# Regrouping 24 units of linear attention feeding a gated product, with two more transposes on the DMA queue and a reordered opening

## The chip, the cores and the metric

The kernel runs on one core of one Trainium2 chip. The metric is device time in microseconds (us), the median of several executions. "Span" is the time that the profiler shows for one execution, some 2 us less.

## The reference

Linear attention with a decay per head, in float32, for 4 batches x 8 heads x 768 positions x 64 dimensions, feeds a bilinear layer over 3072 tokens. In outline, not word for word:

```python
for b in range(nb):                      # blocks of 64 positions
    intra = (qb @ kb.T * Dmask) @ vb     # Dmask: lam ** (i - j) for i >= j
    inter = (qb * lam_pow) @ kv_state
    out[:, :, sl] = intra + inter
    kv_state = lam_block * kv_state + (kb * rev_pow).T @ vb
# ... cut: x = out as 3072 tokens x 512
return (x @ w_a) * (x @ w_b) @ w_out     # 512 -> 1536 -> 512
```

## The kernel before

A **unit** is 128 tokens, so there are 24. For each, the kernel scales q and k (`P`: GpSimd, called POOL below), transposes them (`T` on TensorE from unit 5, or by a transposing DMA from unit `DMA_T_FROM`), forms scores and masks them (`S`), updates and copies the recurrent state (`V`), and forms the attention output (`O`, `O2`; `Q` does it for two units along with the scores of the next two). Then **groups** of one to four units go together through the a and b products (96 matmuls as wide as the group), and unit by unit through the output product. `PLAN` hangs the attention pieces of coming units into slots of the running group; a slot is one of 12 a/b steps, or half an output row later on.

```python
GROUPS = (4, 1, 2, 4, 4, 4, 4, 1)
LOOKAHEAD = (3, 2)
DMA_T_FROM = 9
PLAN = {
    # ... cut: groups 0 and 1
    2: [(0, "V", 6), (1, "T", 7), (1, "P", 8), (4, "T", 8), (4, "P", 9), (6, "S", 7),
        (6, "S", 8), (7, "V", 7), (6, "P", 10), (10, "V", 8),
        (12, "Q", (7, 8, 9, 10)), (12, "P", 11), (13, "V", 9), (14, "P", 12),
        (14, "O2", (9, 10))],
    3: [(3, "S", 11), (3, "S", 12)],     # ... cut: a loop fills groups 3 to 5
}
# ... cut
def prep_k(u):
    make_ks(u, "dve" if u < n0 + 2 else "pool")
    make_qs(u, "pool")
    used["u"] = u + 1
    if u >= DMA_T_FROM:
        qkT = qkT_pool.tile([128, 2, HP, 128], BF16, name="qkT", tag="qkT")
        nc.sync.dma_start_transpose(out=..., in_=...)      # shortened

def prep_v(u):
    make_vb(u, "pool" if u < n0 + 3 else "dve")   # bf16 cast of the values
    pump()                                        # issues the loads that are due
# ... cut
def pieces_O(us, nxt=()):
    kqs = [score_banks() for u in nxt]
    for u in us:
        inter(u)                # full products, 128 x 128 weights
    for u, kq in zip(nxt, kqs):
        scores(u, kq)           # 64-row weights
    for u in us:
        intra(u)                # weights with 64 columns
        xT, col = xTs[u]
        evac_o(u, xT, col)
    if len(us) == 2 and us[0] >= n0 + 5:
        kv_beside(us[1])
    for u, kq in zip(nxt, kqs):
        masks(u, kq)
    # ... cut: state copy
# ... cut: the last row of the last group goes out in pieces of 256, 128, 128 columns
warm(13, 512)                   # idle matmuls while the first loads arrive
# ... cut
for u, at in enumerate((4, 5, 2, 6)):
    U[u]["o"] = ps_bank("o_ps", [128, HP, 128], F32, at=at)
intra(0, True)
evac_o(0, *xTs[0])
intra(1, True)
inter(1)
evac_o(1, *xTs[1], eng="dve")
intra(2, True)
intra(3, True)
inter(2)
evac_o(2, *xTs[2], eng="dve")
inter(3)
evac_o(3, *xTs[3])
```

## Time and profile before

| | before |
|---|---|
| median (lowest to highest), 3 runs | 233.85 us (233.6 to 234.01) |
| profiled span | 231.8 us |
| first a/b matmul starts | 18.59 us |
| TensorE's last matmul ends | 228.69 us |
| last row lands in memory | 230.74 us |

TensorE is busy 97% of the span, so the page is read from TensorE outwards: what each of its matmuls costs from start to start, and what it waits for. The prediction shows those views. Two landmarks split the rest: up to the first a/b product ("the opening") TensorE waits for loads, scalings and casts; after its last matmul ("the tail", 2.05 us here) the last row must be copied and stored.

TensorE's timeline of the opening's end, kernel before (start, busy us, engine, line, operation, shape, count):

```profile
15.36 0.50 PE L366 MATMUL kvd<-vb,scratch 128*128 128x128 bf16 x6
15.79 0.64 PE L352 MATMUL o_ps<-m,vb 128*64 128x128 bf16 x16
16.36 0.40 PE L342 MATMUL o_ps<-scratch,st 128*128 128x128 bf16 x4
16.69 0.68 PE L352 MATMUL o_ps<-m,vb 128*64 128x128 bf16 x16
17.30 0.62 PE L342 MATMUL o_ps<-scratch,st 128*128 128x128 bf16 x8
```

Products with weights of 128\*64 and of 128\*128 take turns: four changes of form (the shape of the weights) from the first line to the last. Four full products at 56 ns would take 0.22 us; from 16.36 to 16.69 they took 0.33.

### The profile page before, as it was taken

Reading aid. Unit: us, or ns where it says so; the run is one execution under the profiler, and the core shown is the slowest. Engines: PE = TensorE matmul, PEld = TensorE weight load, DVE = VectorE, ACT = ScalarE, POOL = GpSimd, SP = SyncE. Lnnn points to the kernel's source line nnn. Section 1 sums busy time; section 2 is a strip of 40 time slices with the busy share of each in tenths; the row PEclk is TensorE's granted clock in tenths of the full one; section 3 lists DMA queues with packets and bytes.
Section 4 is the critical chain, followed back from the end, with each engine's and each line's share of the span. In section 5 each row is a group of like instructions: output and inputs, shape, how many; then the busy total and the mean of one; then the engine's idle time right before and its main releaser. Section 6 shows DMA issues by size and latency. Waiting matters only on the chain.

```text
span 231.8 us, 4520 instructions
## 1 busy us (share of the span) xinstructions
PE 225.2 (97%) x1775; PEld 124.6 (54%) x1775; DVE 115.9 (50%) x204; ACT 91.1 (39%) x172; POOL 50.6 (22%) x65
## 2 busy tenths in 40 slices
PE   7799999999999999999999999999999999999994
PEld 2474444449698554454544454544454544444494
DVE  0896566636469726684334484235583323332050
ACT  3585754066463342333233332333332233332251
POOL 6070000248373333445000543001200000000000
PEclk9999999999999999999999999999999999999999
DMA  4999999999999999998759997229300220000311
GB/s 151 303 283 351 348 364 293 295 207 223 185 225 176 224 208 209 209 197 190 270 189 200 220 182 121 91 96 205 65 3 0 91 93 0 1 0 5 130 49 48
DMA packets 96389, 38.84 MB, mean 168 GB/s; under 512 B 83312, under 2 KB 91888, under 8 KB 96368
## 3 DMA queue, kind: packets, MB, share of 16 engines
q1 hardware_dynamic: 96224, 38.54, 72.9%
q8 instruction: 14, 0.23, 0.4%
q14 instruction: 7, 0.06, 0.1%
q10 hardware_dynamic: 144, 0.00, 0.0%
HBM read 28.32 MB, written 6.29 MB: 149 GB/s over the span
## 4 chain that ended last, share of the span: by engine, by line
PE 92%; DMA 3%; ACT 2%; SPq 1%; DVE 0%; issue 0%
PE a_ps L435 27%; PE b_ps L435 27%; PE op L467 27%; DMA k<-in_k_dram 3%; PE o_ps L352 3%; PE kq L310 2%; PE o_ps L342 2%; PE kvd L366 2%; PE tps L296 1%; ACT o_kept L458 1%; SPq L209 1%; PE kq L578 1%; ACT xT L359 0%; PE kv L366 0%; PE tk L542 0%; DVE scratch L531 0%
## 5 line engine op out<-in xcount | busy, mean ns | idle before, releaser
L447 DVE TENSOR_TENSOR ab<-a_sb,b_ps 128x512 bf16<-128x512 bf16 (+2 forms) x96 | 52.3, 552 | 77.9 <-PE b_ps L435 56.9
L435 PE MATMUL a_ps<-xT,wa_sb 128*128 128x512 bf16 (+2 forms) x384 | 77.2, 326 | 0.6 <-ACT xT L359 0.6
L435 PE MATMUL b_ps<-xT,wb_sb 128*128 128x512 bf16 (+2 forms) x384 | 77.2, 326 | 0.0
L442 ACT CAST a_sb<-a_ps 128x512 bf16<-128x512 f32 (+2 forms) x96 | 45.6, 481 | 63.1 <-PE a_ps L435 61.5
L467 PE MATMUL op<-wo_sb,ab 128*128 128x512 bf16 (+2 forms) x312 | 65.6, 363 | 0.0
L435 PEld LDWEIGHTS <-wb_sb 128*128 128x128 bf16 x384 | 34.5, 98 | 28.7
L435 PEld LDWEIGHTS <-wa_sb 128*128 128x128 bf16 x384 | 33.7, 98 | 29.1 <-POOL wa_sb L162 0.6
L467 PEld LDWEIGHTS <-ab 128*128 128x128 bf16 x312 | 28.8, 98 | 29.9
L327 DVE TENSOR_TENSOR m<-kq,lotri 128x512 bf16<-128x512 f32 x47 | 29.3, 682 | 18.1 <-PE kq L310 17.8
L259 POOL TENSOR_TENSOR qk<-kf,lp_k 128x512 bf16<-128x512 f32 x18 | 18.9, 1049 | 74.7 <-DMA kf<-in_k_dram 47.3
L264 POOL TENSOR_TENSOR qk<-qf,lp_q 128x512 bf16<-128x512 f32 x20 | 22.0, 1099 | 23.4 <-DMA qf<-in_q_dram 23.4
L462 ACT COPY o_sb<-op 128x512 f32<-128x512 f32 (+2 forms) x19 | 10.3, 541 | 34.0 <-PE op L467 34.0
L359 ACT CAST xT<-o_ps 128x512 bf16<-128x512 f32 x22 | 12.0, 590 | 17.9 <-PE o_ps L352 17.5
L398 DVE TENSOR_TENSOR st<-kvd,bdiag 128x512 bf16<-128x512 f32 x18 | 12.3, 682 | 4.9 <-PE kvd L366 3.8
L273 DVE CAST vb<-vf 128x512 bf16<-128x512 f32 x17 | 9.4, 553 | 0.0
L298 ACT COPY qkT<-tps 128x1024 bf16<-128x1024 bf16 x5 | 5.1, 1012 | 9.9 <-PE tps L296 9.9
L197 PE MATMUL idle<-idle_sb 128*128 128x128 bf16 (+1 forms) x31 | 7.2, 372 | 1.3 <-DVE idle_sb L192 1.3
L352 PE MATMUL o_ps<-m,vb 128*64 128x128 bf16 x192 | 7.9, 222 | 0.0
L273 POOL CAST vb<-vf 128x512 bf16<-128x512 f32 x7 | 4.7, 666 | 14.0 <-DMA vf<-in_v_dram 14.0
L342 PEld LDWEIGHTS <-st 128*128 128x128 bf16 x80 | 5.4, 98 | 2.8
L310 PE MATMUL kq<-qkT 64*128 64x128 bf16 x160 | 6.6, 218 | 0.0
L352 PEld LDWEIGHTS <-vb 128*64 128x64 bf16 x192 | 5.8, 109 | 1.4
(57 smaller groups left out, 87.4 us busy)
## 6 DMA issues: line engine op xcount, KB each, us to landing
vf<-in_v_dram SPq DMA_DIRECT2D x24, 256.0 KB, 4.9
qf<-in_q_dram SPq DMA_DIRECT2D x20, 256.0 KB, 4.4
kf<-in_k_dram SPq DMA_DIRECT2D x20, 256.0 KB, 4.6
out_dram<-o_sb SPq DMA_DIRECT2D x16, 256.0 KB, 2.0
wst<-in_moe_w_a_dram SPq DMA_DIRECT2D x6, 512.0 KB, 8.7
wst<-in_moe_w_b_dram SPq DMA_DIRECT2D x6, 512.0 KB, 8.8
wst<-in_moe_w_out_dram SPq DMA_DIRECT2D x6, 512.0 KB, 8.5
out_dram<-o_kept SPq DMA_DIRECT2D x7, 256.0 KB, 2.5
```

The source lines that it names most:

```text
L259: eng_of(eng).tensor_mul(qk[:, 1], raw.pop((u, "k")), lp_k[:, u % NB].to_broadcast([128, H, D]))
L264: eng_of(eng).tensor_mul(U[u]["qk"][:, 0], raw.pop((u, "q")), lp_q[:, u % NB].to_broadcast([128, H, D]))
L273: eng_of(eng).tensor_copy(vb, vf)
L310: nc.tensor.matmul(kq[i][:, hp, :], lhsT=d["kT"][p, hp, :], rhs=d["qT"][p, hp, :], start=True, stop=True, skip_group_check=True)
L327: nc.vector.tensor_mul(m, kq[i], lotri_bc)
L352: nc.tensor.matmul(d["o"][p, hp, :], lhsT=d["vb"][:, 2 * hp + i, :], rhs=d["m"](i, hp), start=(first and hp == 0), stop=True, skip_group_c ...
L359: nc.scalar.copy(xT[:, :, col:col + BLK], o_ps)
L398: nc.vector.tensor_mul(st[:].rearrange("p hp i d -> p hp (i d)"), ps[:].rearrange("p hp i d -> p hp (i d)"), bdiag_bc)
L435: nc.tensor.matmul(ps[:, :gt], lhsT=w_sb[:, s, f * 128:(f + 1) * 128], rhs=xT[:, s, :gt], start=(s == 0), stop=(s == KS - 1))
L442: nc.scalar.copy(a_sb[:, :gt], ps[:, :gt])
L447: nc.vector.tensor_mul(ab[:, f, :gt], a_sb[:, :gt], ps[:, :gt])
L467: nc.tensor.matmul(op[:, lo:hi], lhsT=ab[:, f, t * 128:(t + 1) * 128], rhs=wo_sb[:, f, lo:hi], start=(f == 0), stop=(f == FC - 1))
```

## The change

Its intent: take 16 transposes off TensorE by giving units 7 and 8 to the DMA queue, spread the deadlines of units 7 to 12 by groups of 2, 2 and, at the end, 3, and shorten the opening by ordering its products, masks and evacuations so that less waits for the last values.

```diff
-GROUPS = (4, 1, 2, 4, 4, 4, 4, 1)
+GROUPS = (4, 1, 2, 2, 4, 4, 4, 3)
-DMA_T_FROM = 9
+DMA_T_FROM = 7
 # ... cut
-    2: [(0, "V", 6), (1, "T", 7), (1, "P", 8), (4, "T", 8), (4, "P", 9), (6, "S", 7),
-        (6, "S", 8), (7, "V", 7), (6, "P", 10), (10, "V", 8),
-        (12, "Q", (7, 8, 9, 10)), (12, "P", 11), (13, "V", 9), (14, "P", 12),
-        (14, "O2", (9, 10))],
-    3: [(3, "S", 11), (3, "S", 12)],
+    2: [(0, "V", 6), (1, "P", 8), (4, "P", 9), (9, "P", 10), (10, "S", 7), (10, "S", 8),
+        (11, "V", 7), (13, "P", 11), (14, "O2", (7, 8)), (15, "P", 12)],
+    3: [(1, "S", 9), (1, "S", 10), (2, "V", 9), (5, "Q", (9, 10, 11, 12)), (6, "P", 13),
+        (8, "V", 11), (9, "P", 14), (12, "O2", (11, 12))],
+    4: [(3, "S", 13), (3, "S", 14)],
 }
-for _g, _u in ((3, 11), (4, 15), (5, 19)):
+for _g, _u in ((4, 13), (5, 17)):
 # ... cut: the last groups' slots; qkT buffers 5 -> 6; LOOKAHEAD switches one unit earlier
-        if len(us) == 2 and us[0] >= n0 + 5:
+        if len(us) == 2 and us[0] >= n0 + 3:
             kv_beside(us[1])
 # ... cut: the same condition for its state copy
-    for u in range(n0):
+    for u in range(n0 - 1):
         make_vb(u, "pool")
 # ... cut
-    for hps in ((0, 1), (2, 3)):
-        for u in range(3):
-            kv_part(u, hps)
-            if hps[0]:
-                kv_copy(u, sts[u], ("act", "act", "dve")[u])
+    make_vb(3, "pool")
+    for u in range(2):
+        kv_part(u, (0, 1))
+    for u in range(2):
+        kv_part(u, (2, 3))
+        kv_copy(u, sts[u], "act")
+    kv_part(2, range(HP))
+    kv_copy(2, sts[2], "dve")
 # ... cut
     intra(2, True)
+    inter(2)
+    evac_o(2, *xTs[2])
     intra(3, True)
-    inter(2)
-    evac_o(2, *xTs[2], eng="dve")
     inter(3)
-    evac_o(3, *xTs[3])
+    xT, col = xTs[3]
+    o3 = U[3].pop("o")
+    nc.scalar.copy(xT[:, 0:2, col:col + BLK], o3[:, 0:2])
+    nc.vector.tensor_copy(xT[:, 2:4, col:col + BLK], o3[:, 2:4])
```

More of the change, by code (lines that the diff above doesn't have):

```diff
@@ L57 @@
          (12, "P", _u + 5), (13, "V", _u + 2), (16, "Q", (_u + 2, _u + 3, _u + 4, _u + 5))])
-PLAN[3] += [(_s, "W", None) for _s in range(12, 19)]
-PLAN[5] = [(_s, _n, (21, 22, 23) if _us == (21, 22, 23, 24) else _us)
-           for _s, _n, _us in PLAN[5] if _us != 24]
-PLAN[6] = [(4, "O", 23)]
+PLAN[4] += [(_s, "W", None) for _s in range(9, 16)]
+PLAN[6] = [(1, "P", 23), (4, "V", 21), (7, "Q", (21, 22, 23)), (12, "O", 23)]
 @with_exitstack
@@ L93 @@
     prep_pool = ctx.enter_context(tc.tile_pool(name="prep", bufs=6))
-    qkT_pool = ctx.enter_context(tc.tile_pool(name="qkT", bufs=5))
+    qkT_pool = ctx.enter_context(tc.tile_pool(name="qkT", bufs=6))
     msk_pool = ctx.enter_context(tc.tile_pool(name="msk", bufs=4))
@@ L182, in pump @@
                     return
-            elif c >= used["u"] + LOOKAHEAD[used["u"] > 9]:
+            elif c >= used["u"] + LOOKAHEAD[used["u"] > 8]:
                 return
@@ L424, in pieces_O @@
             masks(u, kq)
-        if len(us) == 2 and us[0] >= n0 + 5 and us[1] % NB < NB - 1:
+        if len(us) == 2 and us[0] >= n0 + 3 and us[1] % NB < NB - 1:
             kv_copy(us[1], kv["ps"])
```

## The prediction

> **What bounds the kernel now.** I read the page's shares first, then who waited for whom on TensorE, then the chain of waits, then single stretches of the timeline. Busy shares and slices of the page:
>
> ```profile
> span 231.8 us, 4520 instructions
> PE 225.2 (97%) x1775; PEld 124.6 (54%) x1775; DVE 115.9 (50%) x204; ACT 91.1 (39%) x172; POOL 50.6 (22%) x65
> ...
> PE   7799999999999999999999999999999999999994
> ...
> PEclk9999999999999999999999999999999999999999
> DMA  4999999999999999998759997229300220000311
> ```
>
> TensorE is busy in every slice but the first two and the last (a slice is 5.8 us); no other engine passes 50%. The DMA row is full up to slice 18 (about 104 us): no bound while TensorE stays full, but the resource the change leans on. TensorE's complete list of waits (us in total, times, longest):
>
> ```profile
> PE idle L197 <- DVE idle_sb L192: 1.3, 1, 1.3
> PE tq L542 <- DVE scratch L531: 0.8, 4, 0.2
> PE tk L542 <- DVE scratch L531: 0.7, 2, 0.4
> PE a_ps L435 <- ACT xT L359: 0.6, 2, 0.5
> PE tn L562 <- ACT scratch L553: 0.2, 1, 0.2
> ```
>
> All of it lies before 18.6 us except 0.2 us at 51.8. So after the opening only fewer TensorE cycles save time, and any new wait costs its full length. What a kind of matmul costs is its pace, not its listed duration, for these overlap. From the chain of waits (start, us, what):
>
> ```profile
> 62.78 0.44 PE a_ps L435 x4
> 63.22 0.44 PE b_ps L435 x4
> ...
> 64.75 0.45 PE tps L296 x8
> ...
> 84.69 0.86 PE b_ps L435 x4
> ```
>
> Four 512-column matmuls pace 0.864 us (216 ns each), four 256-column ones 0.437 (109 ns), eight 128-column transposes 0.45 (56 ns). In the one-unit group the timeline has four 128-column products every 0.224 us (56 ns).
>
> **What the Trainium skill says.** "TensorE: Matmul & The Clock Gate", section "Wait — 56ns, not 53.3ns?", gives 55.6 ns start to start for 128 columns and 215.7 for 512 when warm; the trace agrees (56, 216). The same page under "Back-to-back issue gap" gives about 81 and 131 ns for load-and-multiply streams; the trace contradicts that, and I use the trace. "Advanced Engine Details and Errata", "X-Bar Transpose (TRN2)", says a transposing DMA runs about as fast as a plain one; 15 of them here take a median 4.3 us to land and, in the saturated stretch, add about 0.85 us to the landing series (73.26, 74.09, 74.94), against 1.15 for a 256 KB load. Fair agreement.
>
> **The change, part by part.**
>
> 1. *Groups.* Old: five groups of 4, one of 2, two of 1. New: four of 4, one of 3, two of 2, one of 1. Each group has 96 a/b matmuls of its width. Old: 5 x 96 x 0.216 + 96 x 0.109 + 2 x 96 x 0.056 = 103.7 + 10.5 + 10.8 = 125.0 us. New: 4 x 20.7 + 96 x 0.163 (384 columns, an estimate between the measured widths) + 2 x 10.5 + 5.4 = 82.9 + 15.6 + 21.0 + 5.4 = 124.9 us. The output products are per unit, unchanged. Worth 0: narrow groups are not inefficient here. What moves is deadlines: units 7 and 8 alone are due at about 83 us, and 9 to 12 at about 101, where now 7 to 10 are due at 83.66 and 11 to 14 at 119.
>
> 2. *Units 7 and 8 by DMA.* Removes 16 transposes x 56 ns = **0.90 us** of TensorE, on the path, and two 1.01 us evacuations of ScalarE, off it. Adds two transposing DMAs. For unit 8 the state update goes from 4 to 8 half-size products; the timeline has both at about 0.22 us, so 0.
>
> 3. *Opening.* The stretch that ends it, from the timeline of before:
>
> ```profile
> 15.08 0.62 POOL L273 CAST vb<-vf 128x512 bf16<-128x512 f32 x1 [0.47 <-DMA vf<-in_v_dram]
> ...
> 15.40 1.51 ACT L396 CAST st<-kv 64x256 bf16<-64x256 f32 x4 [0.50 <-PE kv L366]
> 15.66 1.16 POOL L325 TENSOR_TENSOR m<-scratch,lotri 128x512 bf16<-128x512 bf16 x1
> ...
> 17.95 0.59 ACT L359 CAST xT<-o_ps 128x512 bf16<-128x512 f32 x1 [0.43 <-PE o_ps L342]
> ...
> 18.59 1.89 PE L435 MATMUL a_ps<-xT,wa_sb 128*128 128x512 bf16 x8 [0.45 <-ACT xT L359]
> ```
>
> Now: unit 3's values are cast ahead of the POOL mask, so the mask ends at 16.82; ScalarE's state copies start at 15.40; the last evacuation is one 0.59 us cast. After: the mask can start when its source is done (14.90) and ends at 16.07, the cast at 16.69. Unit 0's and 1's products precede unit 2's, so the copies run 14.90 to 16.40. The 24 products run without the pause for unit 2's values, ending near 15.5 instead of 15.7. Unit 2 then goes through at 16.4 to 16.9, unit 3 at 16.9 to 17.4. DVE (masks to 16.21, state 0.68, unit 1's 0.69) is free at 17.6, ScalarE (units 0 and 2, 0.59 each) at 17.6; the two halves take about 0.37 (ScalarE's 256-column cast) and 0.42. The first a_ps starts near 18.1: **0.5 us** gained. Weights allow it: the second a-chunk is cast by 21.48, needed at 22.27 - 0.5; the second b-chunk by 23.34, needed at 23.99 - 0.5. Both just hold.
>
> 4. *What is given back.* I followed the order of issue on the DMA queue, with the landings that the trace matches to each issue. Two transposes more, at 2.1 us each of the queue's issuing, come ahead of units 11 and 12. Estimates from loads landing 3.6 to 4.9 us after issue, two scalings of 1.04 us on POOL, then the transpose (4.8 us): unit 7 lands at 65.6 and 8 at 71.1 (their scores come at about 71.7); unit 12's values at 81.0 (78.9 before); its transpose at 87 (86.1 before). In the second group of two, VectorE has unit 12's cast ahead of everything: done at 81.5 to 81.9. Then two products (0.35), four masks at 0.61 us pace, a product, a state copy and two products bring it to 86.7 to 87.1, when the accumulator of slot 4 comes free. TensorE, at the packed pace, wants that bank for unit 9's output at about 86.3. So a **new wait of 0.4 to 0.8 us**, say 0.6; unit 12's scores follow near 88, just after its transpose. Sum: -0.90 - 0.5 + 0.6 = -0.8 us; 233.85 - 0.8 = 233.05. I go to 232.9, as a slot plan tuned on the chip would probably have taken out part of that wait.
>
> **The rivals.**
>
> - *No new wait.* TensorE stayed full before with loads just ahead of it: 72 us from 40 to 112 with 71.83 busy. If VectorE gets through in time, the gain is 1.4 us: 232.4. For it: deadlines of 9 and 10 move later. Against it: four masks and a state copy now sit in a phase where slots are 0.87 us, not 1.73.
> - *The DMA queue becomes the bound between 70 and 90 us.* A transpose waits in line for POOL and holds up every load behind it:
>
> ```profile
> SPq L282 <- POOL qk L264: 5.5, 7, 2.7
> ...
> SPq L282 <- POOL qk L259: 1.4, 1, 1.4
> ```
>
>   Should values 12 or transpose 12 land 1.5 us later than estimated, VectorE, in order, and then TensorE stop as long: 234.4. Lateness would have to reach 5 us for a loss of 2%.
> - *The opening gains nothing*, because weights set the pace there: 233.4 with the wait of point 4. Against it: above, both chunks still come first.
>
> **Range and chances.** Transposes -0.9 are sure to within 0.1; the opening is -0.5, give or take 0.3; the wait 0 to 1.5. Hence 231.8 to 234.1. A gain over 2% needs 4.7 us, three times all that I can find; a loss over 2% needs a stall of 6. So 0.01, 0.97, 0.02.
>
> **What would show it.** Transposes on TensorE 24 instead of 40 after the opening, DMA transposes 17 instead of 15; a_ps first at about 18.1; a/b time unchanged in sum; TensorE's waits with a new entry of 0.4 to 0.8 us between 82 and 90, on VectorE or a bank, and no other. Wrong if the opening's a_ps doesn't move, if TensorE waits for a transpose or a cast held by its load, or if TensorE idles at a group's edge or in the three-unit tail.

## The result, and the profile after

The changed kernel took 234.21 us (233.88 to 235.01, five runs) against 233.85 in the same rounds. Executions over 1.5% slower than the fastest of the same kernel are left out of the means. Ratios here are the mean time of one kernel's runs over the mean of the other's of the same rounds, so not quite the ratio of these medians: 1.0023, with a 95% interval of 1.0002 to 1.0044. So nothing was gained: 1.3 us more than the 232.9 predicted, just above the range.

The page of the kernel after, busy shares and slices:

```profile
span 232.4 us, 4469 instructions
...
PE 223.3 (96%) x1742; PEld 127.6 (55%) x1763; DVE 115.6 (50%) x204; ACT 89.6 (39%) x171; POOL 50.6 (22%) x65
...
DMA  4999999998999999999999629990222000220012
```

TensorE's busy sum is 1.9 us less, yet the span is 0.6 us longer. The sum is no measure here: 21 matmul records are missing in this trace (1742; the kernel e1 below, with the same instructions in another order, shows 1763, and 225.3 us busy), so I read starts. The DMA row stays full up to slice 21 but for one 8; before, it had a dip to 8, 7, 5 in slices 18 to 20 (the first slice is 0). TensorE's waits, kernel after (us in total, times, longest):

```profile
PE kq L308 <- DMA qkT<-qk: 0.5, 1, 0.5
...
PE o_ps L340 <- DVE ab L445: 0.4, 1, 0.4
```

These two are new: one score block waits for a transposing DMA, one output accumulator for VectorE. Both are between 86 and 89 us. (The view also has 0.5 us of "issue" ahead of output products; e1, with all records, has none.) TensorE's timeline there, kernel after:

```profile
87.48 0.61 PE L340 MATMUL o_ps<-qkT,st 128*128 128x128 bf16 x8 [0.44 <-DVE ab L445]
88.03 0.40 PE L308 MATMUL kq<-qkT 64*128 64x128 bf16 x8
88.90 0.40 PE L308 MATMUL kq<-qkT 64*128 64x128 bf16 x8 [0.48 <-DMA qkT<-qk]
```

The eight score matmuls at 88.03 are unit 11's, those at 88.90 unit 12's. Busy times overlap, so a bracket understates a pause. From the starts of the single matmuls in the trace, 0.60 us was lost before 87.48 and 0.65 before 88.90. Another 0.09 goes at 82.5 to a change of form: from the last 256-column a/b product to the first score product it is 0.205 us, against 0.109 within the form. The changed kernel has 40 changes after its first a/b product, the kernel before 39. Together 1.34 us. The chain of waits says why unit 12 was late (start, us, what):

```profile
76.70 4.61 DMA kf<-in_k_dram
...
81.46 1.04 POOL qk L257
82.51 1.19 POOL qk L262
83.72 5.14 DMA qkT<-qk
```

Unit 12's keys land at 81.30, POOL scales k and q, the transpose is issued at 83.72 and lands at 88.86. VectorE's timeline, kernel after, explains the other wait:

```profile
82.30 0.49 DVE L271 CAST vb<-vf 128x512 bf16<-128x512 f32 x1 [2.12 <-DMA vf<-in_v_dram]
82.71 0.74 DVE L445 TENSOR_TENSOR ab<-a_sb,b_ps 128x256 bf16<-128x256 bf16 x2
83.37 2.47 DVE L325 TENSOR_TENSOR m<-kq,lotri 128x512 bf16<-128x512 f32 x4
...
86.09 0.68 DVE L396 TENSOR_TENSOR st<-kvd,bdiag 128x512 bf16<-128x512 f32 x1
86.70 1.07 DVE L445 TENSOR_TENSOR ab<-a_sb,b_ps 128x256 bf16<-128x256 bf16 x3
```

VectorE stands idle for 2.12 us ahead of unit 12's cast, whose values come by the same queue. Then everything queues: two products, four masks, a product, the state, and the product that frees the accumulator.

The opening, PE and evacuation rows of the timeline of the kernel after:

```profile
15.85 0.64 PE L350 MATMUL o_ps<-m,vb 128*64 128x128 bf16 x16
16.42 0.40 PE L340 MATMUL o_ps<-scratch,st 128*128 128x128 bf16 x4
16.75 0.41 PE L350 MATMUL o_ps<-m,vb 128*64 128x128 bf16 x8
...
17.77 0.40 PE L340 MATMUL o_ps<-scratch,st 128*128 128x128 bf16 x4
18.20 0.37 ACT L638 CAST xT<-o_ps 128x256 bf16<-128x256 f32 x1
18.61 0.42 DVE L639 CAST xT<-o_ps 128x256 bf16<-128x256 f32 x1 [1.06 <-ACT xT L638]
18.62 1.91 PE L433 MATMUL a_ps<-xT,wa_sb 128*128 128x512 bf16 x7 [0.24 <-ACT xT L638]
```

The attention products start no earlier (15.85 for 15.79), now change form six times instead of four, and the two halves of the last evacuation run one after the other. The first a/b matmul starts at 18.62.

The accounts of the two profiled executions, from starts of matmuls and landings of stores in the traces:

| term | predicted | measured |
|---|---|---|
| opening (first a/b start) | -0.5 | +0.03 (18.59 to 18.62) |
| transposes on TensorE | -0.90 | -0.89 (2.23 to 1.34 us in all) |
| a/b time of the groups | 0 | 0 (96 of 384 columns took 15.60 us, estimated 15.6) |
| wait for VectorE at an accumulator | +0.6 | +0.60 |
| wait for unit 12's transpose | 0 | +0.65 |
| one more change of form, at 82.5 | 0 | +0.09 |
| TensorE's last matmul | -0.8 | +0.48 (228.69 to 229.17) |
| tail (last matmul to last landing) | not priced | +0.17 (2.05 to 2.22) |

### The profile page after: what moved, and what is told of

It is laid out like the page before. It is cut to its first block, busy times and chain, and to the rows that moved or that the text cites. A ratio compares the mean times of both kernels' runs of the same rounds, so it can differ in the third digit from the quotient of the medians.

```text
span 232.4 us, 4469 instructions
## 1 busy us (share of the span) xinstructions
PE 223.3 (96%) x1742; PEld 127.6 (55%) x1763; DVE 115.6 (50%) x204; ACT 89.6 (39%) x171; POOL 50.6 (22%) x65
## 4 chain that ended last, share of the span: by engine, by line
PE 85%; DMA 8%; SPq 2%; ACT 1%; issue 1%; POOL 1%; DVE 0%; POOLq 0%; ACTq 0%
PE a_ps L433 26%; PE b_ps L433 25%; PE op L465 24%; DMA k<-in_k_dram 3%; PE o_ps L350 3%; DMA qkT<-qk 2%; PE kq L308 2%; DMA kf<-in_k_dram 2%; PE o_ps L340 2%; PE kvd L364 1%; SPq L280 1%; ACT o_kept L456 1%; SPq L207 1%; PE tps L294 1%; POOL qk L262 1%
## 5 line engine op out<-in xcount | busy, mean ns | idle before, releaser
L445 DVE TENSOR_TENSOR ab<-a_sb,b_ps 128x512 bf16<-128x512 bf16 (+3 forms) x96 | 52.3, 552 | 75.9 <-PE b_ps L433 68.4
L433 PE MATMUL a_ps<-xT,wa_sb 128*128 128x512 bf16 (+3 forms) x377 | 76.6, 325 | 0.8 <-ACT xT L638 0.2
L433 PE MATMUL b_ps<-xT,wb_sb 128*128 128x512 bf16 (+3 forms) x382 | 77.0, 325 | 0.1
L440 ACT CAST a_sb<-a_ps 128x512 bf16<-128x512 f32 (+3 forms) x96 | 45.7, 481 | 65.9 <-PE a_ps L433 54.9
L465 PE MATMUL op<-wo_sb,ab 128*128 128x512 bf16 (+2 forms) x300 | 64.2, 362 | 0.9 <-issue 0.5
L433 PEld LDWEIGHTS <-wb_sb 128*128 128x128 bf16 x384 | 36.0, 98 | 26.6
L433 PEld LDWEIGHTS <-wa_sb 128*128 128x128 bf16 x384 | 35.3, 98 | 27.3 <-issue 0.8
L262 POOL TENSOR_TENSOR qk<-qf,lp_q 128x512 bf16<-128x512 f32 x20 | 21.5, 1074 | 22.9 <-DMA qf<-in_q_dram 22.9
L296 ACT COPY qkT<-tps 128x1024 bf16<-128x1024 bf16 x3 | 3.0, 1012 | 8.9 <-PE tps L294 8.9
```

Source lines behind the costliest of these rows:

```text
L262: eng_of(eng).tensor_mul(U[u]["qk"][:, 0], raw.pop((u, "q")), lp_q[:, u % NB].to_broadcast([128, H, D]))
L433: nc.tensor.matmul(ps[:, :gt], lhsT=w_sb[:, s, f * 128:(f + 1) * 128], rhs=xT[:, s, :gt], start=(s == 0), stop=(s == KS - 1))
L440: nc.scalar.copy(a_sb[:, :gt], ps[:, :gt])
L445: nc.vector.tensor_mul(ab[:, f, :gt], a_sb[:, :gt], ps[:, :gt])
L465: nc.tensor.matmul(op[:, lo:hi], lhsT=ab[:, f, t * 128:(t + 1) * 128], rhs=wo_sb[:, f, lo:hi], start=(f == 0), stop=(f == FC - 1))
```

## The experiments

Kernels sent together shared a chip and its runs of the kernel before, whose medians were 233.63 to 233.82. The theory: what the transposes gave was paid back as waits around 82 to 90 us, because the DMA queue now carries two more transposes ahead of unit 12; the opening's term does not exist. A rival: the loss lies elsewhere (the groups, the tail, the added DMA itself), and the waits are only where it surfaces.

### e1: unit 12's deadline two slots later

```diff
-    3: [... (5, "Q", (9, 10, 11, 12)), (6, "P", 13),
+    3: [... (6, "P", 13), (7, "Q", (9, 10, 11, 12)),
```

> The changed kernel with one edit: in the fourth group the combined piece for units 9 to 12 comes after slot 7 instead of slot 5, 1.75 us later. Theory A (the transpose of unit 12, which landed at 88.86 us, and VectorE, late by 0.60 us, stop TensorE by 1.34 us in all between 82 and 90 us): both waits vanish, the scores of unit 12 come near 89.5 us, and the time is 234.2 - 1.2 = 233.0 us. Rival B (the loss lies elsewhere, or the masks of units 11 and 12, now later, stop TensorE before the output piece of slot 12): 234.2 us, or a new wait after 90 us.

Both waits between 82 and 90 went, and TensorE ended at 228.19 instead of 229.17: 0.98 us, for 1.25 of waits and 0.05 in the opening, less two new pauses of 0.16 at 91.1 and 91.7, where ScalarE's two evacuations and VectorE's masks and state stand ahead of the next casts and products. But the time was 233.82 (233.25 to 233.95), ratio 0.9991 (0.9977 to 1.0006): the same as before. TensorE's gain was lost after its end: the tail took 2.91 us. By the timelines of the output stores, the first of the last five was issued 0.98 us earlier than in the changed kernel (223.60 for 224.58), but the last only 0.27 (229.37 for 229.64): its issuing was held up. The DMA records name the cause. TensorE fetches its own instructions by DMA, 16 KB as one packet, 14 times in an execution. In e1 one such fetch took one of the 16 DMA engines from 227.09 to 228.91. Of the 128 packets (2 KB) of row 22's store, 120 had started by 227.76, the last eight only from 228.90; the store took 4.27 us to land instead of 2.0, and the last row's three pieces stood behind it. So the theory held for TensorE, and there was a second place of loss that I had not priced.

### e2: unit 12's cast on POOL

```diff
-        make_vb(u, "pool" if u < n0 + 3 else "dve")
+        make_vb(u, "pool" if u < n0 + 3 or u == 12 else "dve")
```

> The changed kernel with the cast of unit 12's values on POOL instead of VectorE, which sat idle 2.12 us for that load and then came to the masks late. Theory A (what ends the stall is the landing of unit 12's transpose near 88.9 us; the VectorE wait lies in front of it and is absorbed): the wait of the output product falls from 0.60 us start to start to 0.3 or less, the wait for the transpose grows by as much, and the time stays at 234.2 within 0.15 us. Rival C (each wait costs on its own): 0.4 to 0.6 us less, 233.7 us.

234.24 us (233.81 to 235.01), ratio 1.0018 (1.0000 to 1.0036). The time is as expected, but not for the reason expected: both waits were shorter, 0.35 us for VectorE and 0.5 for the transpose from start to start, as the transpose also landed earlier (88.39), and TensorE ended 0.47 us earlier; a tail of 2.70 took that back. This can't be put down to the edit: run again (r1 below), the unedited changed kernel also waited only 0.38 us for VectorE. What the run does show is that 0.35 us stays with the cast gone. Four masks, a product, the state and a product still stand on VectorE from 83.03 on, ahead of the accumulator.
Whether a shorter VectorE wait alone would be absorbed by the transpose stays undecided, because the transpose moved too.

### e4: units 7 and 8 transposed on TensorE again

```diff
-DMA_T_FROM = 7
+DMA_T_FROM = 9
-    2: [(0, "V", 6), (1, "P", 8), (4, "P", 9), ...
+    2: [(0, "V", 6), (1, "T", 7), (1, "P", 8), (4, "T", 8), (4, "P", 9), ...
```

> The changed kernel with its groups, but units 7 and 8 transposed by TensorE as before. Theory A: the DMA queue has two transposes less ahead of unit 12, whose transpose lands near 86 to 87 us; both waits fall to under 0.3 us together (-1.1), the 16 transposes cost 0.89 us: 234.0 us, no different from either kernel within 0.3. Rival D (the four masks in slots of 0.87 us are the cause, whatever the queue does): the VectorE wait of 0.6 us remains, and the time is 234.5 us or more.

234.0 us (233.93 to 234.11), ratio 1.0004 (0.9991 to 1.0017). Unit 12's transpose landed at 86.54 instead of 88.86, TensorE's wait for it disappeared, and the wait for VectorE was 0.35 us: so rival D was right about that much, whatever the queue does, and the other 0.25 of the changed kernel's 0.60 goes with the late cast (its masks began at 83.37, those of e2 and r1 at 83.03 and 83.00). TensorE ended at 229.37, 0.20 later than in the changed kernel: in this pair of executions, of the 0.89 us that the two DMA transposes take off TensorE some 0.7 came back. Two executions of the changed kernel itself ended 0.23 apart, so this is rough. Part of the 2.3 us by which unit 12's transpose moved is scatter: with the changed kernel's order of the queue it landed between 87.08 (x3) and 88.86 in nine executions. So the two transposes account for 0.5 to 2.3, if e4's single landing is typical.

### e5 and x8: the two DMA transposes in the old groups

e5 is the kernel before with `DMA_T_FROM = 7`, six qkT buffers, and the scores of units 7 and 8 two slots later:

```diff
-    2: [(0, "V", 6), (1, "T", 7), (1, "P", 8), (4, "T", 8), (4, "P", 9), (6, "S", 7),
-        (6, "S", 8), (7, "V", 7), (6, "P", 10), (10, "V", 8),
+    2: [(0, "V", 6), (1, "P", 8), (4, "P", 9), (8, "S", 7),
+        (8, "S", 8), (9, "V", 7), (6, "P", 10), (10, "V", 8),
```

> The kernel before with its groups (4,1,2,4,4,4,4,1) and units 7 and 8 transposed by DMA, their scores moved from slot 6 to slot 8 of the third group. The 16 transposes are worth -0.89 us. Theory A (two more transposes in the DMA queue set everything behind them back by about 3 us): the transpose of unit 10 lands near 77.5 to 78.2 us, but its scores are due near 75.5 us, so TensorE waits 1.5 to 2.5 us there and the time is 234.4 to 235.4 us. Rival (the queue catches up, as the DMA engines had slack): 232.95 us.

234.52 us (234.03 to 234.92), ratio 1.0032 (1.0016 to 1.0049). The waits view of e5:

```profile
PE kvd L366 <- DVE st L398: 1.4, 1, 1.4
```

That is a stall of my own making: the slot shift put two state copies behind four masks on VectorE. It says nothing of the queue. x8 takes it out: unit 8's state update goes beside its output products, as in the changed kernel.

```diff
-        (8, "S", 8), (9, "V", 7), (6, "P", 10), (10, "V", 8),
+        (8, "S", 8), (9, "V", 7), (6, "P", 10),
-        if len(us) == 2 and us[0] >= n0 + 5:       # twice
+        if len(us) == 2 and us[0] >= n0 + 3:
```

> As e5_dma_only (groups of the kernel before, units 7 and 8 by DMA), but the state update of unit 8 comes beside its output, as in the changed kernel, so that two state copies no longer follow each other behind four masks, which is where e5_dma_only lost 1.5 us. Theory A: the transpose of unit 10 lands near 77.4 us and its scores are due near 76.9 us: a wait of 0.3 to 1 us, in all 233.8 - 0.9 + 0.3 to 1 = 233.2 to 233.9 us. If the DMA queue has slack here: 232.9 us.

234.03 us (233.44 to 234.68), ratio 1.0015 (0.9999 to 1.0032). Its waits view:

```profile
PE kq L310 <- DMA qkT<-qk: 1.2, 2, 0.8
```

With the old groups TensorE waits for transposes of units 9 and 10, which now land at 76.31 and 77.56. So in either grouping tried, the DMA transposes' 0.89 us turns into waits for later transposes.

### e6: the new opening alone

The kernel before with the opening's lines of the diff above, and nothing else.

> The kernel before with the new opening alone (order of products, cast after the mask on POOL, split evacuation). The prediction on record gave it 0.5 us: 233.35. What the two traces suggest instead: the new order alternates six times instead of four between full products and products with 64 columns of weights, each alternation 0.20 us start to start instead of 0.03 to 0.06, and that eats the gain: 233.85 within 0.15 us, first a_ps product no more than 0.1 us from 18.59.

233.76 us (233.64 to 234.11), ratio 0.9996 (0.9981 to 1.0011); the first a/b matmul started at 18.47. The opening is worth nothing that these runs resolve. (The 0.20 us in the expectation is a misreading: by the starts in both traces, the change from one form to the other takes 0.15 us for 128-column products, against 0.056 within a form, so it costs 0.09.)

### x3: the instruction fetches shifted

If fetches come after a fixed count of TensorE instructions, more and shorter idle matmuls at the start must move them all. From e1:

```diff
-    warm(13, 512)
+    warm(48)          # 48 of 128 columns
```

> The changed kernel with the combined piece at slot 7, and 48 idle matmuls of 128 columns instead of 13 of 512 in the wait for the first load: 70 more TensorE instructions, so that each instruction fetch of 16 KB comes some 35 matmuls earlier. Theory E: the last fetch (at 227.09 us, 1.82 us long) held one DMA engine with its share of row 22's store, whose last eight packets started at 228.90, and the last store landed 2.9 us after TensorE's end where the kernel before took 2.05. Now the fetch comes near 222 us, the last landing is about 2.05 us after TensorE's end, and the time is 233.8 - 0.85 = 232.95 us. Rival F (two full stores and three pieces so close together are slow by themselves): the last landing stays 2.7 to 2.9 us after TensorE's end, 233.8 us.

232.85 us (232.82 to 232.91), ratio 0.9962 (0.9949 to 0.9976): 0.97 us below e1's median, or 0.7 by the two ratios, as the two ran on different chips, with TensorE's end unmoved (228.20 against 228.19). The last fetch came at 222.18 instead of 227.09, and the tail was 1.94. The spread of six executions fell from 0.70 us to 0.09. So the tail of the three-unit group was a collision of a store with a fetch, shown by moving the fetches alone.

### x7: another shift

From e1, a shift by 13 matmuls instead of 35:

```diff
-    warm(13, 512)
+    warm(26, 256)
```

> The changed kernel with the combined piece at slot 7 and 26 idle matmuls of 256 columns: 13 more, so the last fetch comes some 13 matmuls earlier than the one at 227.09 us, near 226.2 us, and if it takes 1.0 to 1.8 us ends at 227.2 to 228.0. It still holds one engine's share of row 22's store, but that engine has time to catch up before the last piece. Theory E: row 22's store lands 1 us late or so, the last landing is 1.95 to 2.3 us after TensorE's end, time 232.9 to 233.2 us. Rival F (the position of the fetch doesn't matter): 233.8 us.

232.88 us (232.83 to 232.89), ratio 0.9962 (0.9950 to 0.9974); the last fetch came at 225.35 and was over at 226.30, between the bulk of two stores (the first landed in 2.16 us instead of 2.02), and the tail was 1.94. It is the fetch's place, not the number of idle matmuls.

### x5: the same shift in the kernel before

> Control: the kernel before with the same 48 idle matmuls instead of 13 wide ones. Its last fetch (227.62 us) ends just ahead of its first output piece, and its last landing is 2.05 us after TensorE's end. If the edit acts only through the last fetch, nothing changes here: 233.8 us within 0.2, last landing 2.0 to 2.1 us after TensorE's end, first a_ps product within 0.1 us of 18.59. If the edit is worth something by itself (warmer clock, earlier fetches elsewhere), this is faster too.

The edit is that of x3, in the kernel before. 234.68 us (234.19 to 234.99), ratio 1.0040 (1.0024 to 1.0056): 0.9 us slower by the ratio, not unchanged as expected. As a control it failed, but it showed what the reordered opening is good for. The first fetch now came at 13.63 instead of 18.18 and delayed unit 3's values to 16.13 (15.03 before). POOL's and TensorE's timeline, x5 (old opening):

```profile
16.18 0.61 POOL L273 CAST vb<-vf 128x512 bf16<-128x512 f32 x1 [1.56 <-DMA vf<-in_v_dram]
16.76 1.15 POOL L325 TENSOR_TENSOR m<-scratch,lotri 128x512 bf16<-128x512 bf16 x1
17.96 0.49 PE L352 MATMUL o_ps<-m,vb 128*64 128x128 bf16 x11 [0.91 <-POOL m L325]
```

The same rows for x3 (new opening), whose values were as late (16.39):

```profile
14.99 1.15 POOL L323 TENSOR_TENSOR m<-scratch,lotri 128x512 bf16<-128x512 bf16 x1 [0.38 <-ACT scratch L322]
16.44 0.61 POOL L271 CAST vb<-vf 128x512 bf16<-128x512 f32 x1 [0.30 <-DMA vf<-in_v_dram]
```

In the old order the mask stands behind the late cast and TensorE waits, to an a/b start of 19.69; in the new order the mask is done first, and the start is 18.60. The new opening saves 1.1 us when values are late, and nothing when they are not.

### x6, and both again: the shift in the changed kernel

> The changed kernel with nothing but the 48 idle matmuls (the fetches come some 35 matmuls earlier; the combined piece stays at slot 5). Its waits for VectorE and for the transpose, 1.34 us, should remain, and only the tail should change: last landing 1.94 instead of 2.22 us after TensorE's end, so 234.2 - 0.3 = 233.9 us, and runs closer together than the 1.1 us over which those of the changed kernel spread, if the spread comes from the last fetch. If the 1 us gained by x3_fetch against the late piece alone came from something else in the body, this run too would gain about 1 us: 233.2 us.

The edit is that of x3, in the changed kernel. 233.26 us (233.10 to 233.62), ratio 0.9980 (0.9969 to 0.9992): more gain than the tail alone should give. So I ran the changed kernel and x6 once more, together on another chip.

> The changed kernel, unedited, on the same chip and in the same rounds as the next run. Expected: 234.2 us within 0.3, spread of 0.8 us or more among its runs; waits for VectorE and the transpose of unit 12 of 1.2 to 1.4 us start to start together; last fetch within 1.2 us of TensorE's end and a last landing 2.2 to 2.9 us after it.

> x6_after_fetch again, unedited, beside the changed kernel. Its profiled run was the slowest of its five (233.62 against 233.26). If the tail is all that the shifted fetches change, it is 0.3 to 0.9 us faster than the changed kernel beside it, the size of that kernel's tail over 1.94 us, with the same waits of about 1.2 us in the body. If the fetches also free the body, the waits fall to 0.8 us or less.

The changed kernel again: 234.09 us (233.21 to 234.87), ratio 0.9997 (0.9973 to 1.0021). x6 again: 233.17 us (233.15 to 233.29), ratio 0.9970 (0.9953 to 0.9987). The difference of 0.92 us lies in two places. The profiled tails of the changed kernel were 2.22 and 3.20, those of x6 both 1.94. And the wait for unit 12's transpose varied: 0.65 and 0.79 us in the changed kernel, 0.83 and 0.13 in x6, as the transpose landed at 88.86, 88.62, 88.66 and 87.92. In the first of these a fetch at 84.82 lasting 1.31 us delayed the load of unit 13's values, queued just ahead of the transpose: it landed 5.76 us after its issue, against the usual 4.6. That may make up to 1.1 us of unit 12's lateness. But the kernel before has such a fetch too (at 83.94, with unit 12's transpose landing 5.89 us after its issue), so it is nothing new; and in x6 no fetch lies there, and it was still late once; a fetch at 81.08 delayed unit 11's landing. What moves this landing by a microsecond is left open. The wait for VectorE was 0.60 us in the first of the four executions and 0.35 to 0.38 in the other three.

### x4: everything that helped

From x3, `intra(2)` ahead of `inter(1)` in the opening, so that the products change form four times instead of six:

```diff
     intra(1, True)
+    intra(2, True)
     inter(1)
     evac_o(1, *xTs[1], eng="dve")
-    intra(2, True)
     inter(2)
```

> As x3_fetch, and in the opening unit 2's 64-column products go ahead of unit 1's full products: four alternations between the two kinds instead of six. At 0.15 us each over the normal pace this is 0.3 us of TensorE, of which a wait for the POOL mask (ends 16.2 us) and for ScalarE's evacuation of unit 2 may take back half: first a_ps product 0.1 to 0.3 us earlier than in x3_fetch, time 232.65 to 232.85 us if the last fetch stays clear of the stores. If alternation isn't the cost, no difference.

232.78 us (232.72 to 232.90), ratio 0.9960 (0.9945 to 0.9975). The first a/b matmul started at 18.42 instead of 18.60, and TensorE ended 0.17 earlier. The 44 attention products took 1.92 us from first to next block, against 2.15 in the changed kernel. TensorE then waited 0.3 us for the cast of the first weight chunk, so here the weights set a floor at about 18.4 (that cast began at 17.75, against 17.25 in the changed kernel). This version is faster than the kernel before, by 0.85 us on the same chip: its interval excludes 1, and it is still under 1%. It was not run beside the changed kernel.

## Why the prediction was wrong

The time stayed within 2%, as foreseen, but no gain of 0.9 us came. Three steps failed and one term was left out, each worth some tenths and all in the same direction. Two of the text's own signs of being wrong came: the opening's first a/b product did not move, and TensorE waited for a transpose.

**Right by their own working.** Transposes: -0.89 against -0.90. Groups: 0, with the 384-column estimate at 15.60 us. The wait for VectorE, 0.60 of "0.4 to 0.8", at the accumulator of unit 9's output and for the reason given: cast, masks and state in order on VectorE, ahead of a product. (The cast was done at 82.8, not 81.5 to 81.9.) So this much of the trade was priced as it came in the profiled execution: 0.9 off, 0.6 back. The size was partly luck: in three other executions of the same plan the wait was 0.35 to 0.38, and e2 and e4 show 0.35 without the late cast. Masks, state and products make that much without it.

**Point 3, the opening: predicted -0.5, measured +0.03.** Two of its sentences failed. "The 24 products run without the pause for unit 2's values, ending near 15.5": there was no such pause. The stretch from the first of these products to the first attention product took 1.60 us in both traces. The 0.26 us that this is over 24 times 0.056 lies, in both kernels, in a pause of 0.16 after the second product, where a mask of VectorE ends just before TensorE goes on (14.43 and 14.47 in the kernel before), and in a change of form at the end: 0.15 us from the last product of one form to the first of the next, against 0.056 within a form. And "unit 2 then goes through at 16.4 to 16.9" counted products, not changes; two more cost 0.19. The working is then +0.06 for the start, +0.19 for the changes, -0.22 because the last evacuation before the first a/b product is a half (0.37 for 0.59): +0.03. x4 shows the term by removing two changes: -0.18. The Trainium skill could have told me: "TensorEngine Tiling (Array Packing)", "Key Properties", says that changing the tiling mode drains TensorE. The trace agrees that a change costs time: the 0.15 us. The third rival, weights as the pace, was not what held it, since the first a/b product waited for the evacuation; x4, whose weights came 0.5 us later, met that limit at 18.42.

**Point 4, the queue: the wait for unit 12's transpose, predicted 0, measured 0.65.** The step was "its transpose at 87" and "unit 12's scores follow near 88, just after its transpose". It landed at 88.86. Worked back, 87 less 4.8 us for the transpose and two scalings of 1.04 puts unit 12's keys at 80.1. They landed at 81.30, 3.3 us later than before (77.96); from there to the issue took 2.42 us and the transpose 5.14. So 1.2 of the 1.9 us was lost upstream in the queue, and 0.3 each in scaling and landing. The mis-sized term is what two more transposes do to the landings behind them: 0.9 us in the estimate, 2.8 in this execution (86.08 to 88.86), at least 1.0 in nine. Why so much, and why it scatters, is not shown. The second rival had the mechanism ("should values 12 or transpose 12 land 1.5 us later than estimated, ... TensorE stop as long"). That its 234.4 is near 234.21 is partly luck: it has the opening's 0.5 us of gain in it, and a stop of 1.5 where 0.65 came. e4 shows the dependence from the other side (two transposes less, landing 0.5 to 2.3 us earlier, no wait for it), e1 by moving the deadline.

**A term that was not in the sum: the tail.** I took the last 2 us as fixed. The three-unit group puts two whole rows and three pieces into the last 5.1 us of issuing, where the kernel before issued the three pieces alone (its last whole row went out at 221.33), and a fetch falls among them. It cost 0.17 us in one profiled execution and 1.15 in another, and accounts for a good part of the changed kernel's spread of 1.1 us. The text did say that it would be wrong "if TensorE idles at a group's edge or in the three-unit tail"; it was the DMA engine, after TensorE.

**The last step down, 233.05 to 232.9**, for a slot plan "tuned on the chip", had no measurement behind it, and went the wrong way. With the opening at 0 and the transpose's wait in, the working would have said 234.2.

What stays open: why unit 12's transpose lands anywhere between 87.1 and 88.9 us; and whether VectorE's wait alone would be hidden behind it.

## What to carry to other kernels

Work moved from a full engine to a full queue is not removed: before counting the gain, find the next thing in that queue with a deadline, and give it slack for the scatter of its landings (1.8 us over nine executions here). Count changes between forms of matmul as well as matmuls. And when a kernel's end is a burst of stores, look at what else uses the DMA engines at that moment; here moving the instruction fetches gained more than all of the change, though the same shift lost 0.9 us in the kernel before.

## What the Trainium skill lacked or had wrong

- "Runtime: NRT & Kernel Launch", "Instruction fetch mechanics", has the blocks of 16 KiB and calls their cost mostly hidden. The size agrees (14 packets of 16 KB for TensorE). It lacks that a fetch holds one of the 16 DMA engines for 0.9 to 1.95 us, so that a store or load beside it lands late: row 22's store took 4.27 us instead of 2.0, and moving the fetches was worth 0.7 to 1.0 us in the changed kernel and in e1.
- "TensorEngine Tiling (Array Packing)", "Key Properties", gives no figure for the drain at a change of mode: 0.15 us start to start between 128x128 and 128x64 weights with 128 columns, for 0.056 without a change.
- "TensorE: Matmul & The Clock Gate", "Back-to-back issue gap": about 81 ns for 128 columns and 131 for 512 in streams of loads and matmuls; measured 56 and 216.
- Pages give bandwidths for transposing DMAs, but none that I found says what one adds to a saturated queue of loads: mostly 0.8 to 1.0 us for a unit's 256 KB (the step from the landing before it to its own, in both kernels), and two of them made unit 12's transpose land 0.5 to 2.3 us later.
